# Fourier mixing and an ELU feed-forward on one core: complex product by three real products, units between the halves of the first layer, ELU in halves

## The chip, the cores and the metric

One core of a Trainium2 chip runs one program. The metric is the device time of one execution in microseconds, and the kernel before takes 918.88 us (median of 3 runs, 918.64 to 919.0). The five engines that the text speaks of are PE (TensorE, matmuls, with its weight loads shown as PEld), DVE (VectorE), ACT (ScalarE), POOL (GpSimd) and SP (SyncE, which here only issues transfers).

## The reference

There are 8 batches of 3008 tokens by 256 channels. Each batch goes through a Fourier transform over its tokens, a complex 256x256 matrix product with a bias, soft thresholding, and the inverse transform; then all 24064 tokens go through a two-layer feed-forward with an ELU.

```python
X = rfft(x, axis=1);  Xr, Xi = X.real, X.imag
Yr = Xr @ w_r - Xi @ w_i + b_r
Yi = Xr @ w_i + Xi @ w_r + b_i
Yr = sign(Yr) * max(abs(Yr) - 0.01, 0)      # the same for Yi
y = irfft(Yr + 1j * Yi, n=3008, axis=1)     # (8, 3008, 256)
h = y.reshape(24064, 256) @ w_in            # (24064, 2048)
g = where(h > 0, h, exp(min(h, 0)) - 1)
out = g @ w_out                             # (24064, 256)
```

## The kernel before

**The two parts.** The transform of 3008 = 47 x 64 points is done in stages of matmuls, each followed by a copy out of PSUM. Their pieces are called units. A (`unit_A`, 6 for a batch) is the 47-point stage, written to DRAM (`DA`) and read back as `Z` in another order (`load_Z`). X (`unit_X`, 8) is the 64-point stage, copied to `XT`. M (`unit_M`, 12) is the complex product with the weights. B (`unit_B`, 6) and Y (`unit_Y`, 8) are the inverse stages, with a second trip through DRAM (`DB`, `load_Bs`). Y leaves `yT`, the input of the feed-forward.

**The feed-forward** runs in 376 iterations (47 for a batch). A block is 512 tokens, and 8 iterations go over its 2048 hidden columns, 256 at a time. `front` makes the hidden values of one iteration with 4 matmuls into `hps` (two PSUM banks), ACT takes the exponential into `Et`, DVE or POOL take its minimum, and DVE writes the result to `gT`. Two iterations later (`LAG = 2`) `back` multiplies `gT` by `w_out` with 8 matmuls. `gT` is a ring of three tiles.

**The order of the work** is written out by hand. Batch 0's transform and the tables stand ahead of the loop. Inside it `plan(b)` gives each of the 47 iterations (slots 0 to 46) at most one unit: the late Y of batch b, then X, M and B of batch b+1, A of batch b+2, and the first two Y of batch b+1 (called n). PE runs, for each iteration, the unit (list `f0`), the 4 matmuls of `front`, and the 8 of `back`. A second list, `f1`, holds loads and small steps. In slot 3 of batch 0 it holds `gate`, a POOL copy that waits until `Z` of batch 1 has landed, and the first `load_x` of batch 2 behind it, also issued by POOL.

**Engines of the ELU before.** An iteration without a unit (`free`) has two exponentials of 128x512 on ACT (L735), the minimum in halves on POOL (L763) and two DVE steps (L751). One with a unit other than M has one exponential of 128x1024 (L740), the minimum on DVE (L765) and one DVE step (L753). One with an M has a Relu and an exponential of 128x1024 on ACT (L737, L738) and one DVE step (L751). `psH` holds two tiles of two banks each, and `psF` one of two banks for the units, lent to every third free iteration.

**M before.** For each half of a pair, four matmuls of 512 columns (L193: two for the real part of the input, two for the imaginary, each with [w_r, w_i] or [-w_i, w_r]); DVE adds the bias (L203); POOL clips (L211) and subtracts (L212). Where batches 1 to 7 are meant these are the M inside the loop; batch 0 has its own `first_M`, which the change leaves alone.

**Startup.** `unit_A(1, ...)` runs ahead of the loop and puts two of its three tiles into the slots of the `gT` ring (`shifted`), so that the first writes of `gT` wait until `DA<-A` has been read out.

Of the kernel before, what the change touches and what calls it, by code (L numbers as in the profile page):

```python
# [14 lines left out]

# [8 lines left out]
NJ = 24  # L24
# [5 lines left out]
def kernel(  # L30
# [31 lines left out]
    wcat_s = constp.tile([P, 2, 2 * D], BF16, name="wcat_s")  # L62
    w_in_s = constp.tile([P, 2, DFF], BF16, name="w_in_s")
    w_out_p = constp.tile([P, NFT, E + 16], F32R, name="w_out_r")
    w_out_r = w_out_p[:, :, 0:E]
    bias_bc = constp.tile([P, 2 * D], F32, name="bias_bc")
    bias_p = constp.tile([P, 2 * D], BF16, name="bias_p")
# [11 lines left out]
    zp = ctx.enter_context(tc.tile_pool(name="zp", bufs=1))  # L79
    wk2 = ctx.enter_context(tc.tile_pool(name="wk2", bufs=2))  # L80
# [10 lines left out]
    TB = 512  # L91
# [37 lines left out]

    def unit_A(b, u, alone=False, on_dve=False, ahead=False):  # L130
        ci, uu = u // 2, u % 2
        if uu == 0:
            if ahead and ci > 0:
                A_of[b, ci] = shifted(ci - 1, 8 * D, BF16, "A").rearrange("p (n d) -> p n d", d=D)
# [14 lines left out]
        evac(  # L149
            A[:, 4 * uu : 4 * uu + 4, :].rearrange("p n d -> p (n d)"),  # L150
            ps[:].rearrange("p a b -> p (a b)"), on_dve,
        )
        j0 = 8 * ci
        if alone:
            j0 += 4 * uu
            nc.sync.dma_start(dav[:, j0 : j0 + 4, :], A[:, 4 * uu : 4 * uu + 4, :])
        elif uu == 1:
            nc.sync.dma_start(dav[:, j0 : j0 + 8, :], A[:])
# [8 lines left out]
    def unit_X(b, u, alone=False, on_dve=False):  # L167
# [14 lines left out]
        evac(xv, pv, on_dve)  # L182
# [23 lines left out]

    def unit_M(b, q, i):
        if i == 0:
            mps_of[b, q] = unit_ps("mps", False)
        yb, clip = m_group(b, q, i, mps_of[b, q][:, i, :])  # L210
        nc.gpsimd.tensor_scalar(clip[:], yb, LAM, -LAM, ALU.min, ALU.max)  # L211
        nc.gpsimd.tensor_tensor(Y_of[b, q][:, i, :], yb, clip[:], ALU.subtract)  # L212
# [21 lines left out]
    def unit_B(b, v, alone=False, on_dve=False):  # L234
# [16 lines left out]
        o = 4 * (v % 2)  # L251
        Bv = Bz[:, o : o + 4, :].rearrange("p (q s) d -> p s q d", s=2)
        psv = ps[:].rearrange("p s (q d) -> p s q d", d=D)
        if on_dve:
            nc.scalar.copy(Bv[:, :, 0], psv[:, :, 0])
            nc.vector.tensor_copy(Bv[:, :, 1], psv[:, :, 1])
        else:
            nc.scalar.copy(Bv, psv)  # L258
        if alone:
            k0 = 4 * v  # L260
            nc.sync.dma_start(
                DB_of[b][k0 : k0 + 4].rearrange("k p d -> p k d"), Bz[:, o : o + 4, :]
            )
        elif v % 2:
            k0 = 8 * (v // 2)
            nc.sync.dma_start(DB_of[b][k0 : k0 + 8].rearrange("k p d -> p k d"), Bz[:])
# [8 lines left out]
    def unit_Y(b, u, alone=False, on_dve=False):  # L275
# [11 lines left out]
        evac(  # L287
            yT[:, dt, w * WT : w * WT + WT].rearrange("p (r j) -> p r j", j=8),
            psv[:, :, 0 : 2 * N1].rearrange("p j r -> p r j"), on_dve,
        )  # L290
# [23 lines left out]
    with tc.tile_pool(name="stagep", bufs=1) as stagep:  # L314
# [35 lines left out]
        w_r_f = row("w_r_f", [P, 2, D])  # L350
        w_i_f = row("w_i_f", [P, 2, D])
# [217 lines left out]
    SHIFT = (0, 32, 16)  # L569

    def shifted(k, n_, dt, name):

        k %= 3
        o = SHIFT[k] * n_ // (8 * TB)
        w_ = n_ + 64 * n_ // (8 * TB)
        t = late1.tile([P, w_], dt, name=name, tag=f"gT{k}")
        return t[:, o : o + n_]
# [110 lines left out]
    for u in range(2):  # L688
# [7 lines left out]
        tc.tile_pool(name="psH", bufs=2, space=bass.MemoryType.PSUM, reuse_waits="tile")  # L696
# [19 lines left out]
    def front(i, third, on_act, halves):  # L716
        blk, fp = divmod(i, NPAIR)
        if third:
            hps = psF.tile([P, 2, TB], F32, name="hps", tag="fps")
        else:  # L720
            hps = psH.tile([P, 2, TB], F32, name="hps", tag="hps")
        for s in range(2):
            ft = 2 * fp + s
            for b, t0, c0, c1 in sorted(pieces(blk * TB, TB), key=lambda z: z[3] - z[2]):
                for dt in range(2):
                    nc.tensor.matmul(  # L726
                        hps[:, s, c0:c1], lhsT=w_in_s[:, dt, ft * P : ft * P + P],
                        rhs=yT_of[b][:, dt, t0 : t0 + c1 - c0],
                        start=(dt == 0), stop=(dt == 1),
                    )  # L730
        Et = late3.tile([P, 2, TB], F32, name="Et", tag="Et")
        E_ = Et[:]
        if halves:
            for s in range(2):
                nc.scalar.activation(E_[:, s], hps[:, s], AF.Exp)  # L735
        elif on_act:
            nc.scalar.activation(E_, hps[:], AF.Relu, scale=-1.0)  # L737
            nc.scalar.activation(E_, E_, AF.Exp, scale=-1.0)  # L738
        else:
            nc.scalar.activation(E_, hps[:], AF.Exp)  # L740
        return hps, Et

    late_elu = []

    def finish_elu():
        for i, hps, Et, whole, halves in late_elu:
            gT = shifted(i + 2, 2 * TB, F32R, "gT").rearrange("p (s t) -> p s t", s=2)
            for s in range(2) if halves else (slice(0, 2),):
                o, h, e = gT[:, s], hps[:, s], Et[:, s]
                if whole:  # L750
                    nc.vector.scalar_tensor_tensor(o, e, -1.0, h, ALU.add, ALU.max)  # L751
                else:
                    nc.vector.scalar_tensor_tensor(o, h, 0.0, e, ALU.max, ALU.add)  # L753
            g_of[i] = gT
        late_elu.clear()

    def elu(i, hps, Et, on_pool, on_act):

        E_ = Et[:]
        if on_pool:  # L760
            for s in range(2):
                eng = nc.vector if i == n - 1 and s == 0 else nc.gpsimd
                eng.tensor_scalar(E_[:, s], E_[:, s], 1.0, 0.0, ALU.min, ALU.max)  # L763
        elif not on_act:
            nc.vector.tensor_scalar(E_, E_, 1.0, -1.0, ALU.min, ALU.add)  # L765
        late_elu.append((i, hps, Et, on_pool or on_act, on_pool))

    def back(i, split):
# [24 lines left out]
        for q in range(nq):  # L793
            copy = nc.vector.tensor_copy if (last and q) or (split and q == 0) else nc.scalar.copy
# [16 lines left out]
    def plan(b):  # L811
# [4 lines left out]
        mid = [("X", u) for u in range(8)] + [  # L816
# [4 lines left out]
        ]  # L821
        if n1 < B:
            lead, seq = int(b == 0), [("y", u) for u in range(2, 6)] + mid
            seq.insert(20 if b else 4, ("y", 6))
            seq.insert(24 if b else 5, ("y", 7))
            xs = (3, 8, 13)
            seq += [("A", 5), ("n", 0), ("n", 1)] if b else [("n", 0), ("n", 1), ("A", 5)]
        else:
            lead, seq = 0, [("y", u) for u in range(2, 8)]
        for t, u in enumerate(seq, lead):  # L830
# [7 lines left out]
            else:  # L838
                f0[t].append(put(u[0], n1, *u[1:]))
            if u == ("A", 1):  # L840
                f1[t] += [(load_Bs, (n1, w)) for w in range(4)]
            if u == ("A", 5) and n2 < B:
                f1[t] += [(load_Z, (n2, s0, s1)) for s0, s1 in ((0, 8), (8, NS))]
        if b == 0:
            f1[3].append((scale_w_in, (3, True, 0)))
# [8 lines left out]
    bare = 0  # L854
    for i in range(n + LAG):
        if i < n:
# [4 lines left out]
            free = not used[r]  # L861
            bare = bare + 1 if free else 0
            calm = free and (i >= n - 2 or (r + 2 < PER and not used[r + 1] and not used[r + 2]))
            for f, a in f0[r]:
                f(*a)
            on_act = any(f is unit_M for f, a in f0[r])
            h = front(i, calm and bare % 3 == 1, on_act, free and i > 0)
        finish_elu()
        if i < n:
            for f, a in f1[r]:  # L870
                f(*a)
            split = i > LAG and (i - LAG) % NPAIR == NPAIR - 1
            if split:
                back(i - LAG, True)
            elu(i, *h, free and i > 0, on_act)
        else:
            split = False
        if i >= LAG and not split:
            back(i - LAG, False)
# [30 lines left out]
```

## Time and profile before

| | before |
|---|---|
| median of 3 runs | 918.88 us (918.64 to 919.0) |
| span of the profiled execution | 916.2 us, granted PE clock 0.997 |
| PE busy | 898.2 us (98%) |
| DVE, ACT busy | 718.1 us (78%), 696.8 us (76%) |
| POOL busy | 313.4 us (34%) |
| DMA, mean over the span | 116 GB/s |

The span runs from the first to the last instruction of one profiled execution. No separate time of that execution is listed; the median of the runs is 2.7 us above the span, which is what lies around it. Matmuls are pipelined, so the mean of one (303 ns for L784) is longer than its share of PE; periods between starts of the same kind are the safer reading.

### The profile page before, as it was taken

To read this page: it belongs to the slowest core of one execution; us is meant where nothing else is said; L and a number is where in the kernel's file an instruction comes from. 1 tells how busy PE (TensorE), PEld (TensorE's weight loads), DVE (VectorE), ACT (ScalarE), POOL (GpSimd) and SP (SyncE) were. 2 spreads that over 40 slices of the span, in tenths; PEclk is the share of its full clock that TensorE was granted. 3 is DMA by queue.
4 is the path that set the end of the run, shared out by engine and by line. 5 is a ranking of instruction groups with operands and counts; after the bars stand their busy time and mean duration, and the time that the engine had idled before them with its cause. 6 is when DMAs were issued, how large, how long until landed. Compare 5 with 4: busy or idle time off the path is not lost.

```text
span 916.2 us, 17270 instructions
## 1 busy us (share of the span) xinstructions
PE 898.2 (98%) x6721; PEld 655.8 (72%) x6721; DVE 718.1 (78%) x891; ACT 696.8 (76%) x850; POOL 313.4 (34%) x438
## 2 busy tenths in 40 slices
PE   8889999999999999999999999999999999999997
PEld 3447667876678766886678766787667866777775
DVE  8759778887788777887788877888778877778775
ACT  6658778778778778787787788878877877766664
POOL 6600440323321342405404153033332134343664
PEclk9999999999999999999999999999999999999999
DMA  8997026621284214732266032752228111321011
GB/s 264 310 264 230 24 71 182 210 63 53 70 233 135 71 47 135 191 113 75 65 192 200 24 94 60 218 160 70 70 71 229 30 42 47 87 76 47 26 46 46
DMA packets 90670, 106.24 MB, mean 116 GB/s; under 512 B 5270, under 2 KB 81308, under 8 KB 87228
## 3 DMA queue, kind: packets, MB, share of 16 engines
q1 hardware_dynamic: 84332, 77.62, 30.3%
q0 software_dynamic: 5968, 27.26, 9.0%
q8 instruction: 52, 0.85, 0.4%
q10 hardware_dynamic: 288, 0.26, 0.1%
q14 instruction: 30, 0.25, 0.1%
HBM read 55.32 MB, written 49.81 MB: 115 GB/s over the span
## 4 chain that ended last, share of the span: by engine, by line
PE 88%; DMA 3%; ACT 3%; DVE 3%; issue 1%; SPq 1%; POOL 0%; ACTq 0%; DVEq 0%; POOLq 0%
PE ps_o L784 36%; PE hps L726 34%; PE mps L193 9%; PE xps L176 2%; PE yps L283 2%; PE bps L245 2%; PE aps L145 2%; DMA Bs<-DB 1%; DMA DA<-A 1%; ACT Et L737 1%; ACT Bz L258 1%; SPq L802 0%; DMA xt<-in_x_dram 0%; DVE gT L751 0%; DMA DB<-Bz 0%
## 5 line engine op out<-in xcount | busy, mean ns | idle before, releaser
L784 PE MATMUL ps_o<-w_out_r,gT 128*128 128x256 f32 x3008 | 482.5, 303 | 0.1
L784 PEld LDWEIGHTS ps_o<-w_out_r,gT 128*128 128x128 f32 x3008 | 406.8, 189 | 50.0 <-DVE osb L795 1.0
L726 PE MATMUL hps<-yT,w_in_s 128*128 128x512 bf16 (+4 forms) x1728 | 390.0, 353 | 3.3 <-DVE gT L753 2.5
L751 DVE SCALAR_TENSOR_TENSOR gT<-Et,hps 128x512 fp32r<-128x512 f32 (+1 forms) x272 | 222.8, 848 | 76.3 <-POOL Et L763 39.3
L753 DVE SCALAR_TENSOR_TENSOR gT<-hps,Et 128x1024 fp32r<-128x1024 f32 x198 | 242.1, 1223 | 18.0 <-DMA DA<-A 2.6
L726 PEld LDWEIGHTS <-w_in_s 128*128 128x128 bf16 x1728 | 141.7, 98 | 130.9 <-issue 23.5
L740 ACT ACTIVATE Et<-hps 128x1024 f32<-128x1024 f32 x198 | 203.9, 1030 | 14.3 <-PE hps L726 8.0
L763 POOL TENSOR_SCALAR Et<-Et 128x512 f32<-128x512 f32 x187 | 111.3, 614 | 224.9 <-ACT Et L735 224.9
L765 DVE TENSOR_SCALAR Et<-Et 128x1024 f32<-128x1024 f32 x198 | 137.0, 692 | 49.5 <-ACT Et L740 42.2
L211 POOL TENSOR_SCALAR clip<-yb 128x512 f32<-128x512 f32 x84 | 51.6, 614 | 319.5 <-DVE yb L203 282.1
L735 ACT ACTIVATE Et<-hps 128x512 f32<-128x512 f32 x188 | 102.1, 595 | 65.1 <-PE hps L726 65.1
L737 ACT ACTIVATE Et<-hps 128x1024 f32<-128x1024 f32 x84 | 86.3, 1027 | 72.6 <-PE hps L726 72.1
L212 POOL TENSOR_TENSOR Y<-yb,clip 128x512 bf16<-128x512 f32 x84 | 107.2, 1276 | 7.0
L738 ACT ACTIVATE Et<-Et 128x1024 f32<-128x1024 f32 x84 | 88.8, 1057 | 2.7
L203 DVE TENSOR_TENSOR yb<-mps,bias_bc 128x512 f32<-128x512 f32 x89 | 61.4, 689 | 36.8 <-PE mps L193 29.8
L128 ACT CAST XT<-xps 128x768 bf16<-128x768 f32 x61 | 48.7, 799 | 16.4 <-PE xps L176 16.4
L128 ACT CAST yT<-yps 128x752 bf16<-128x752 f32 x63 | 49.6, 788 | 14.6 <-PE yps L283 14.5
L193 PE MATMUL mps<-wcat_r,XT 128*128 128x512 bf16 x192 | 58.1, 383 | 0.8 <-DVE XT L126 0.4
L128 ACT CAST A<-aps 128x1024 bf16<-128x1024 f32 x45 | 45.5, 1013 | 16.3 <-PE aps L145 14.6
L193 PE MATMUL mps<-wcat_s,XT 128*128 128x512 bf16 x192 | 57.1, 379 | 0.0
L193 PEld LDWEIGHTS <-XT 128*128 128x128 bf16 x384 | 30.8, 98 | 29.9 <-DVE XT L126 0.7
L258 ACT CAST Bz<-bps 128x1024 bf16<-128x1024 f32 x46 | 46.0, 1000 | 2.6 <-PE bps L245 2.6
(110 smaller groups left out, 412.0 us busy)
## 6 DMA issues: line engine op xcount, KB each, us to landing
xt<-in_x_dram POOLq DMA_DIRECT2D x21, 1024.0 KB, 7.1
out_dram<-osb SPq DMA_DIRECT2D x158, 128.0 KB
Bs<-DB SPq DMA_DIRECT2D x32, 384.0 KB
DA<-A SPq DMA_DIRECT2D x21, 512.0 KB
DB<-Bz SPq DMA_DIRECT2D x21, 512.0 KB
Z<-DA SPq DMA_DIRECT2D x7, 1152.0 KB
Z<-DA SPq DMA_DIRECT2D x11, 384.0 KB
xt<-in_x_dram POOLq DMA_DIRECT2D x6, 512.0 KB, 6.2
```

Of the source, the lines that this page charges most:

```text
L128: nc.scalar.copy(dst, src)
L193: nc.tensor.matmul(ps, lhsT=XT[:, dt, c, o : o + P], rhs=wm[:, dt, :], start=(not biased and m == 0 and dt == 0), stop=(m == 1 and dt == 1),)
L212: nc.gpsimd.tensor_tensor(Y_of[b, q][:, i, :], yb, clip[:], ALU.subtract)
L726: nc.tensor.matmul(hps[:, s, c0:c1], lhsT=w_in_s[:, dt, ft * P : ft * P + P], rhs=yT_of[b][:, dt, t0 : t0 + c1 - c0], start=(dt == 0), sto ...
L735: nc.scalar.activation(E_[:, s], hps[:, s], AF.Exp)
L737: nc.scalar.activation(E_, hps[:], AF.Relu, scale=-1.0)
L740: nc.scalar.activation(E_, hps[:], AF.Exp)
L751: nc.vector.scalar_tensor_tensor(o, e, -1.0, h, ALU.add, ALU.max)
L753: nc.vector.scalar_tensor_tensor(o, h, 0.0, e, ALU.max, ALU.add)
L763: eng.tensor_scalar(E_[:, s], E_[:, s], 1.0, 0.0, ALU.min, ALU.max)
L765: nc.vector.tensor_scalar(E_, E_, 1.0, -1.0, ALU.min, ALU.add)
L784: nc.tensor.matmul(po[q][:, i_ % 2, :], lhsT=gT[:, s, i_ * P : i_ * P + P], rhs=w_out_r[:, ft, :], start=(ft == 0 and i_ % 2 == 0), stop=( ...
```

## The change

1. **M by three products.** For batches 1 to 7 the complex product is formed from K = (Xr - Xi) w_i, P = Xr (w_r - w_i) and Q = Xi (w_r + w_i): real part P + K, imaginary part Q + K. That is six matmuls of 256 columns in place of four of 512. The difference Xr - Xi is a new POOL step (`unit_D`, 128x256 in bf16), made two M ahead. DVE adds b_r to K (128x256) and then K to both parts (128x512). POOL adds b_i - b_r to the imaginary part (128x256), then clips and subtracts as before. Three POOL steps in slots 5 to 7 of batch 0 make the sums of the weights and of the bias.
2. **Units between the halves of the first layer.** PE's order in an iteration is now two matmuls of `front`, the unit, two matmuls of `front`, `back`. The unit's copy out of PSUM is issued later (`later`, `flush`): for units other than M between ACT's two exponentials, for M ahead of part of DVE's queue.
3. **ELU in halves.** `psH` holds four tiles of one bank. Each half has its own exponential and its own DVE step. The minimum is on POOL in all iterations without an M, those with X, B, A or Y among them; with an M it is on ACT (two Relu of 128x512, one exponential of 128x1024); in the first 4 iterations it is on DVE. `psF` is for units alone.
4. **Another plan.** X of the next batch begins in slot 5 (batch 0) or 2 in place of 7 or 4; late Y and some A now stand among the M as fill; the slot of n0 goes from 37 to 43 with the batch. Among M0 to M11 stand 4 other slots for batch 1 (worked on in plan 0), 7 for batch 2, 8, 9 and more for later ones. `load_x` moves to slots 1, 4, 7 (batch 0 keeps 3, 8, 13, and `gate` stays in slot 3).
5. **Memory.** `w_out` loses its 16 padding columns and the `gT` ring its shifts; the tiles of `unit_A(1, ...)` move out of the ring. Of each block's two output copies one is always on DVE.

The core of the diff:

```diff
 def unit_M(b, q, i):
+    k = 2 * q + i
+    XT, Xd, o = XT_of[b], Xd_of.pop((b, k)), k * P
+    ps = unit_ps("mps", False)
+    kp = ps[:, 1, 0:D]
+    for lhs, rhs, dst in (
+        (lambda dt: Xd[:, dt], lambda dt: wcat_r[:, dt, D : 2 * D], kp),
+        (lambda dt: XT[:, dt, 0, o : o + P], lambda dt: wsum[:, 0, dt], ps[:, 0, 0:D]),
+        (lambda dt: XT[:, dt, 1, o : o + P], lambda dt: wsum[:, 1, dt], ps[:, 0, D : 2 * D]),
+    ):
+        for dt in range(2):
+            nc.tensor.matmul(dst, lhsT=lhs(dt), rhs=rhs(dt), start=dt == 0, stop=dt == 1)
...
+    def done():
+        nc.vector.tensor_tensor(Kb[:], kp, bias_bc[:, 0:D], ALU.add)
+        nc.vector.tensor_tensor(
+            two(yb[:]), two(ps[:, 0]), Kb[:].unsqueeze(1).to_broadcast([P, 2, D]), ALU.add
+        )
+    def clip_():
+        nc.gpsimd.tensor_tensor(yb[:, D : 2 * D], yb[:, D : 2 * D], bias_d[:], ALU.add)
+        nc.gpsimd.tensor_scalar(clips[0][:], yb[:], LAM, -LAM, ALU.min, ALU.max)
+    def sub_():
+        nc.gpsimd.tensor_tensor(Y_[:, i, :], yb[:], clips[0][:], ALU.subtract)
+    jobs.append((clip_, lambda: unit_D(b, k + 2), sub_))
...
+            h = front_ps()
+            e = Elu(i, h, "dve" if i < 4 else {"M": "act", "F": "pool"}[kind])
+            front_mm(i, h, 0)
             for f, a in f0[r]:
                 f(*a)
+            front_mm(i, h, 1)
+            if was:
+                was.mix(1 if kind == "M" and len(was.todo) == 2 else 0 if kind == "M" else 2)
+            e.exp(0)
+            if kind != "M":
+                flush()
+            e.exp(1)
+            flush()
+            if was:
+                was.mix()
             for f, a in f1[r]:
                 f(*a)
...
+            if kind == "M":
+                for c_, x_, s_ in todo[:-1]:
+                    x_(); s_()
+                todo[-1][0]()
+                jobs.append(todo[-1])
+            else:
+                e.least(0)
+                for c_, x_, s_ in todo: x_()
+                e.least(1)
+                for c_, x_, s_ in todo: s_()
+            e.mix({"MM": 0, "MF": 0, "FM": 1, "FF": 2}[kind + then])
```

Here `x_` is `unit_D` of two M later, `least` the minimum of a half and `mix` the DVE step of a half.

More of the change, by code (lines that the diff above doesn't have):

```diff
@@ L714, in pieces, with front_ps, front_mm @@
         return out_
-    def front(i, third, on_act, halves):
+    def front_ps():
+        return [psH.tile([P, TB], F32, name="hps", tag="hps")[:] for _ in range(2)]
+    def front_mm(i, hps, s):
         blk, fp = divmod(i, NPAIR)
[L718 to L729, printed above, removed]
-                    )
[L731 to L741, printed above, removed]
@@ L757, in elu @@
[L757 to L768, printed above, removed]
+        ft = 2 * fp + s
+        for b, t0, c0, c1 in sorted(pieces(blk * TB, TB), key=lambda z: z[3] - z[2]):
+            for dt in range(2):
+                nc.tensor.matmul(
+                    hps[s][:, c0:c1], lhsT=w_in_s[:, dt, ft * P : ft * P + P],
+                    rhs=yT_of[b][:, dt, t0 : t0 + c1 - c0],
+                    start=(dt == 0), stop=(dt == 1),
+                )
```

254 lines of the change are left out of this document (170 added, 84 removed), and 4 rows, old and new, of the table mid.

## The prediction, made before the changed kernel ran

> **What bounds the kernel now.** I read the page first: busy shares, the chain that ended last, then the groups by form.
>
> ```profile
> PE 898.2 (98%) x6721; PEld 655.8 (72%) x6721; DVE 718.1 (78%) x891; ACT 696.8 (76%) x850; POOL 313.4 (34%) x438
> PE 88%; DMA 3%; ACT 3%; DVE 3%; issue 1%; SPq 1%; POOL 0%; ACTq 0%; DVEq 0%; POOLq 0%
> L212 POOL TENSOR_TENSOR Y<-yb,clip 128x512 bf16<-128x512 f32 x84 | 107.2, 1276 | 7.0
> L211 POOL TENSOR_SCALAR clip<-yb 128x512 f32<-128x512 f32 x84 | 51.6, 614 | 319.5 <-DVE yb L203 282.1 <-PE hps L726 37.4
> L499 POOL TENSOR_TENSOR v<-v,r 128x47 f32<-128x47 f32 x1 | 0.3, 292 | 0.1
> ```
>
> PE sets the time, so PE time that is removed is worth its full length unless a wait takes its place. POOL is idle for two thirds of the span, and its two-input steps are slow (1.28 us for 512 elements).
>
> The timeline gives the period of each sort of iteration, start to start:
>
> ```profile
> 229.10 0.60 PE L193 MATMUL mps<-wcat_r,XT 128*128 128x512 bf16 x2
> 231.79 0.60 PE L193 MATMUL mps<-wcat_r,XT 128*128 128x512 bf16 x2
> ...
> 504.31 1.03 PE L726 MATMUL hps<-yT,w_in_s 128*128 128x512 bf16 x4
> 499.95 1.04 PE L726 MATMUL hps<-yT,w_in_s 128*128 128x256 bf16 x8
> ```
>
> An M iteration takes 231.79 - 229.10 = 2.69 us. By the same reading a free one takes 1.82 (486.05 to 487.87), one with Y or X 2.17, with A 2.29, with B 2.36. The last two lines show that eight matmuls of 256 columns take as long as four of 512: PE pays by the column.
>
> Last the start of the loop, where PE still waits:
>
> ```profile
> 65.32 1.23 DVE L753 SCALAR_TENSOR_TENSOR gT<-hps,Et 128x1024 fp32r<-128x1024 f32 x1 [2.09 <-DMA DA<-A]
> 72.97 0.51 PE L283 MATMUL yps<-M,Bs 96*128 96x94 bf16 x8
> 76.95 0.18 POOL L599 CAST gate<-Z 96x1 f32<-96x1 bf16 x1 [14.88 <-DMA Z<-DA]
> 77.44 1.83 POOL L117 DMA_DIRECT2D xt<-in_x_dram  x3 [0.32 <-issue]
> 58.00:60.00 2.00, 2.00 (x12) 1.07 (x11) 0.00 (x0) 0.65 (x1) 0.00 (x0) 0.50 1.06 298
> ```
>
> POOL sits in `gate` until 76.95, and nobody minds, since nothing of POOL's is needed so early. The last line is a stretch of 2 us with the granted clock in its third column from the end: half.
>
> **1. M by three products, on PE.** M costs 2.69 - 1.82 = 0.87 us; six times 256 columns are three quarters of four times 512, so 0.22 is saved, 84 times: **-18.3**.
>
> **2. The start: POOL's gate now stands ahead of the ELU.** Iteration 4 is the first whose minimum is on POOL, and POOL reaches it only after slot 3, that is after `gate` and one `load_x`. What `gate` waits for does not move: the same transfers in the same SP order stand ahead of `Z`. So: gate 76.95, issue from 77.44 for 1.83 / 3 = 0.61 to 78.05, first half of the minimum 0.61 to 78.66, DVE's half 0.69 (a row of L751) with a hand-over of 0.03 to 79.38. Only then is the bank free that iteration 6 writes first, and PE, DVE and SP stand behind it. Before, PE stood at that same point (units y2 to y5 and one more done, iteration 6 next) at 72.97: 6.4 lost. The gain that the moved tiles of A would bring (DVE's 2.09 us in the first line) comes before that stall and is swallowed by it, and so is any wait of X0 in slot 5 for the first part of `Z`. Behind the gate the two weight sums (two-input, 512 elements, 1.28 each) delay the minima of iterations 5 and 6: iteration 7 can start at 79.25 + 1.28 + 0.61 + 0.72 = 81.86, against 79.38 + 2.17, iteration 8 likewise: 0.6 in all. After 6 us without work PE's clock should be half for a time, as in the line at 58 to 60 (with its neighbours about 3.4 us at half, at most 1.7 us of work lost); POOL holds PE back there anyway, so I take 0.5 between 0 and 1.7. Sum **+7.5**.
> The Trainium skill, "TensorE: Matmul & The Clock Gate", Part 1, says that an idle window of about 3.4 us halves the clock until a window of work has passed. The trace agrees (0.50 at 58 to 60); by that rule alone this item would be 1.2 more.
>
> **3. POOL among the M of batch 1.** Two-input POOL rows: 292 ns at 47 elements, 1276 at 512, so 2.12 ns an element and 0.73 us at 256. Each M then asks POOL for the difference 0.73, the bias 0.73, the clip 0.61, the subtraction 1.28, and 0.08 between dependent steps (7.0 / 84 in L212): 3.43, where PE needs 2.69 - 0.22 = 2.47. Twelve M put POOL 12 x 0.96 = 11.5 us behind. An iteration without M asks POOL for 1.20 (two halves, back to back) and gives back 1.16 (B) or 0.97 (Y). For batch 1 only four B stand among the M: -4.6. The first two differences are made earlier (-1.5), M11's subtraction delays nothing among them (-1.3), and a difference may be 0.9 late: after an M's matmuls DVE needs 1.11, POOL 1.42 and 0.73, together 3.3, and the M after next wants it 4.3 later. Left: **+3.2**. For batch 2 four B and three Y give back 7.5, and 11.5 - 7.5 - 3.7 = **+0.3**. Later batches have more fill: 0.
> The difference is bf16 in and out, which no two-input row shows. Half the fp32 rate per byte gives 0.45, the price of 512 elements 1.28; the row of L212 already writes bf16 at the fp32 slope, so I take 0.73 and keep both for the range.
>
> **4. Units between the halves.** One more change of kind on PE for each of some 270 units. A costs 2.29 - 1.82 = 0.47 against 0.43 for two matmuls of 512: at most 0.02 for a change, 0 to 5.5; **+1.5**, since X and Y show almost none. ACT runs exponential, unit copy, exponential: 1.19 + 1.01 = 2.20 in the worst case (A), below 2.29, and 2.25 (two Relu of 0.595, L738's 1.06) in an M iteration, below 2.47: hidden; where ACT has an output copy of 0.58 as well, it runs late for an iteration and eats slack. The bank pairs come free within about 2.8 us of a half's matmuls (0.60 + 0.61 + 0.69 and a unit's copy of at most 1.01), and PE returns to them after 3.6 or more: hidden. DVE falls to two halves of 0.69 for most iterations (1.38 of 1.82 or more), with 0.42 + 0.69 for an M: hidden, and `psF` is free 1.1 us after an M's matmuls, 0.7 before the next unit.
>
> **5. The rest.** `load_Bs` of batch 1 is issued two slots earlier against its use, which takes away PE's wait of 0.7 at 151 (a Y for `Bs<-DB`): **-0.7**. Padding and ring shifts: no row shows `back` without them; between rows of one tile place and another `back`'s pace differs by about 1 ns in 118, so 0 +- 3. The last iteration's minimum is no longer split with DVE, hidden by DVE's own half: 0.
>
> Sum on the span: 916.2 - 18.3 + 7.5 + 3.2 + 0.3 + 1.5 - 0.7 = 909.7. With the 2.7 us around it (918.88 - 916.2): **912.4**.
>
> **Rivals.**
> *POOL is dearer, and it is slower.* Place: the M stretches; price: each 0.1 us more on POOL per M costs about 1.2 in batch 1 and 2 each, and less in later ones as fill absorbs it. At 0.2 more (3.63 in all) it is 2.4 + 2.4 + 1.7 + 0.6 = 7, and the gain is gone: this is the point that decides. At 0.3 more it is near 13, so about **924**. For it: the sum stands 5% below the turning point, and two steps of four have no row of their own. Against: rows at 1, 47 and 512 elements lie on a line. Chance 0.2.
> *POOL is cheaper or the start is mild.* The difference at 0.45 takes away item 3 (-3.4): 909; if also PE lost only half of item 2, **905**. For it: bf16 has half the bytes. Against: `gate`'s place in POOL's order is plain. Chance 0.15.
> *ACT becomes the bound.* Halves cost 2 x 0.595 against 1.03 (L735, L740), 0.16 more. In A and B iterations ACT would have 2.2 of 2.3 us; with 0.1 more for each hand-over in 78 of them it is 8 us: **920**. Against: in the trace two halves back to back take 1.08, not 1.19. Chance 0.08.
> The Trainium skill, "Advanced Engine Details and Errata", The Read-Write Bubble, advises instructions of 512 or 1024 elements, because latency is exposed between instructions; it speaks against the halves, and this rival is what it would do here.
> *The saving is not made*, because six weight loads in place of four set PE's pace: PEld's 98 ns for one (L726, bf16) lies under the 0.87 / 8 = 109 ns of 256 columns, so hardly; it would give 912 + 18 = 930, chance 0.02.
>
> **How the numbers follow.** Forecast 0.55, the cases above 0.45. 0.2% (1.8 us) is about what a measurement can tell from no change. Faster by more: 0.51 of the forecast's 0.55 (its spread, from items 2 to 5, is some 906 to 919) and the cheap case's 0.15, 0.66. The same: the forecast's other 0.04, 0.04 of the POOL case and 0.03 of ACT's, 0.11. Slower: the other 0.16 and 0.05 of these two, and 0.02 of the last, 0.23. The range runs from the cheap case to the dear one: 904 to 923.
>
> **What would show it.** PE's M iteration at 2.47 us; POOL at 600 us or more, with rows near 0.73 for the difference and the bias; PE idle for some 6 us before iteration 6's first matmul at about 79.4, released by DVE behind POOL's `gate`; waits of M on the difference in batch 1 (100 to 135 us), few in batch 3 and later. It is wrong if the difference's row is above 0.9, if the stall at 73 to 79 is absent, or if PE waits for ACT throughout.

## The result, and the profile after

The changed kernel takes 906.06 us (median of 4 runs, 905.47 to 907.28); the kernel before, on the same chip, 918.82. The ratio is 0.9864, with a 95% interval of 0.985 to 0.9878. The forecast was 912.4, with a range of 904 to 923. The profiled execution has a span of 904.2 us and took 905.97. For the kernel before no time of the profiled execution is on record; in its later runs, which have both, the time is 1.7 to 1.9 us above the span, so its 916.2 belong to a run of some 918.0. The 2.7 us taken as lying around the span were about 0.9 too many.

The page of the changed kernel, busy shares and the chain that ended last:

```profile
PE 873.7 (97%) x6778; PEld 668.6 (74%) x6889; DVE 654.7 (72%) x1066; ACT 709.6 (78%) x1132; POOL 664.8 (74%) x998
PE 84%; POOL 6%; issue 4%; DVE 3%; DMA 2%; ACT 1%; SPq 0%; ACTq 0%; DVEq 0%; POOLq 0%
```

PE still carries the chain, but POOL, at 0% of it before, now has 6%. POOL's busy time went from 313 to 665 us. Where it went, by the groups of the changed kernel (busy time and mean ns of one behind the bar, then the idle time ahead of them):

```profile
L813 POOL TENSOR_SCALAR Et<-Et 128x512 f32<-128x512 f32 x576 | 351.1, 617 | 166.7 <-ACT Et L808 165.7
L278 POOL TENSOR_TENSOR Y<-yb,clip 128x512 bf16<-128x512 f32 x84 | 108.4, 1290 | 0.3
L274 POOL TENSOR_TENSOR yb<-yb,bias_d 128x256 f32<-128x256 f32 x84 | 61.6, 734 | 13.3 <-DVE yb L266 12.4
L240 POOL TENSOR_TENSOR Xd<-XT 128x256 bf16<-128x256 bf16 x84 | 56.3, 673 | 0.0
L275 POOL TENSOR_SCALAR clip<-yb 128x512 f32<-128x512 f32 x84 | 51.7, 615 | 7.4
```

An M costs POOL 0.673 + 0.734 + 0.615 + 1.290 + 0.09 (7.4 / 84, the gap ahead of the clip) = 3.40 us; the prediction had 3.43. The two rows that it had to draw from a line, 0.73 each, came out at 0.734 in fp32 and 0.673 in bf16.

PE's timeline after, an iteration with M and then, after the dots, one without a unit:

```profile
215.84 0.39 PE L790 MATMUL hps<-yT,w_in_s 128*128 128x512 bf16 x1
216.29 0.38 PE L256 MATMUL mps<-wcat_r,Xd 128*128 128x256 bf16 x2
216.50 0.60 PE L256 MATMUL mps<-wsum,XT 128*128 128x256 bf16 x4
218.31 0.60 PE L790 MATMUL hps<-yT,w_in_s 128*128 128x512 bf16 x2
...
477.81 1.04 PE L790 MATMUL hps<-yT,w_in_s 128*128 128x512 bf16 x3
479.61 1.04 PE L790 MATMUL hps<-yT,w_in_s 128*128 128x512 bf16 x4
```

From first half to first half the M iteration takes 218.31 - 215.84 = 2.47 us, as forecast. The free one takes 1.80; before it was 1.82, and nothing in the sum of the prediction stood for that.

The start of the loop in the timeline after, first PE (in brackets the idle time ahead and what ended it):

```profile
73.03 0.82 PE L192 MATMUL xps<-M,Z 96*128 96x96 bf16 x8 [5.91 <-DMA Z<-DA]
80.29 1.01 PE L790 MATMUL hps<-yT,w_in_s 128*128 128x512 bf16 x2 [3.88 <-DVE gT L825]
```

The same stretch of the timeline, POOL:

```profile
77.79 0.18 POOL L665 CAST gate<-Z 96x1 f32<-96x1 bf16 x1 [16.74 <-DMA Z<-DA]
78.29 0.56 POOL L115 DMA_DIRECT2D xt<-in_x_dram  x1 [0.32 <-issue]
78.88 1.21 POOL L813 TENSOR_SCALAR Et<-Et 128x512 f32<-128x512 f32 x2
```

And two stretches of 2 us from the view by windows (busy time of PE, PEld, DVE, ACT and POOL, then the granted clock, the DMA share and GB/s):

```profile
72.00:74.00 2.00, 0.97 (x9) 0.77 (x10) 0.00 (x0) 0.11 (x1) 0.00 (x0) 0.50 0.99 227
82.00:84.00 2.00, 2.00 (x9) 1.75 (x8) 1.10 (x2) 1.38 (x2) 2.00 (x3) 0.50 0.32 123
```

PE stands twice: 5.91 us for the first part of `Z`, which X0 in slot 5 needs, and then 3.88 us for DVE's half of iteration 4, whose minimum waits on POOL behind `gate` until 78.88. Iteration 6 starts at 80.29 (forecast 79.4). The granted clock, third from the end, is at half in both stretches. By the records it is so from 71.1 to 84.8.

**Where the time went.** A period is the time from the last matmul of one `back` to that of the next. A batch here is the 47 iterations of one plan, so batch 0's M are those that the prediction calls M of batch 1. For each kind of iteration I take the median over batches 1 to 7, before and after:

| kind (number of such iterations) | before | after |
|---|---|---|
| M (84) | 2.687 | 2.467 |
| B (42) | 2.458 | 2.479 |
| A (36) | 2.290 | 2.294 |
| X (56), Y (60) | 2.170, 2.166 | 2.147, 2.140 |
| without a unit (95) | 1.823 | 1.800 |

Medians times numbers change by -22.5 us. What the periods take beyond their medians, PE's waits mostly, goes from 7.9 to 21.1: in batch 0 from 3.2 to 16.5 (13.7 of it in the iterations of X0 to X2), in batches 1 to 7 from 4.8 to 4.6. The first `back` ends 2.1 earlier (a figure of one execution: in the ten variants of the changed kernel below it ends between 62.2 and 64.2, here at 62.3), and -0.3 is left for the tail. The sum is -11.8, and the spans differ by 12.0.

### The profile page after: what moved, and what is told of

It is laid out like the page before. It is cut to its first block, busy times and chain, and to the rows that moved or that the text cites. A ratio compares the mean times of both kernels' runs of the same rounds, so it can differ in the third digit from the quotient of the medians.

```text
span 904.2 us, 18246 instructions
## 1 busy us (share of the span) xinstructions
PE 873.7 (97%) x6778; PEld 668.6 (74%) x6889; DVE 654.7 (72%) x1066; ACT 709.6 (78%) x1132; POOL 664.8 (74%) x998
## 4 chain that ended last, share of the span: by engine, by line
PE 84%; POOL 6%; issue 4%; DVE 3%; DMA 2%; ACT 1%; SPq 0%; ACTq 0%; DVEq 0%; POOLq 0%
PE ps_o L845 36%; PE hps L790 32%; PE mps L256 5%; PE bps L314 3%; PE xps L192 2%; PE aps L158 2%; PE yps L355 2%; POOL Y L278 1%; PE mps L209 1%; POOL yb L274 1%; POOL Et L813 1%; POOL Xd L240 1%; POOL clip L275 1%; DMA Bs<-DB 1%; DMA xt<-in_x_dram 1%
## 5 line engine op out<-in xcount | busy, mean ns | idle before, releaser
L825 DVE SCALAR_TENSOR_TENSOR gT<-Et,hps 128x512 fp32r<-128x512 f32 x752 | 496.9, 684 | 193.6 <-POOL Et L813 168.7
L813 POOL TENSOR_SCALAR Et<-Et 128x512 f32<-128x512 f32 x576 | 351.1, 617 | 166.7 <-ACT Et L808 165.7
L790 PE MATMUL hps<-yT,w_in_s 128*128 128x512 bf16 (+7 forms) x1622 | 418.6, 354 | 6.2 <-DVE gT L825 4.7
L808 ACT ACTIVATE Et<-hps 128x512 f32<-128x512 f32 x584 | 341.7, 603 | 103.3 <-PE hps L790 98.9
L804 ACT ACTIVATE Et<-hps 128x512 f32<-128x512 f32 x168 | 100.6, 599 | 51.9 <-PE hps L790 46.8
L274 POOL TENSOR_TENSOR yb<-yb,bias_d 128x256 f32<-128x256 f32 x84 | 61.6, 734 | 13.3 <-DVE yb L266 12.4
L266 DVE TENSOR_TENSOR yb<-mps,Kb 128x512 f32<-128x512 f32 x84 | 58.1, 692 | 3.0
L240 POOL TENSOR_TENSOR Xd<-XT 128x256 bf16<-128x256 bf16 x84 | 56.3, 673 | 0.0
L265 DVE TENSOR_TENSOR Kb<-mps,bias_bc 128x256 f32<-128x256 f32 x84 | 35.5, 423 | 27.9 <-PE mps L256 27.7
L256 PE MATMUL mps<-wsum,XT 128*128 128x256 bf16 x336 | 50.4, 273 | 0.0
L192 PEld LDWEIGHTS <-Z 96*128 96x128 bf16 x512 | 29.2, 99 | 22.5 <-DMA Z<-DA 7.4
L192 PE MATMUL xps<-M,Z 96*128 96x96 bf16 x512 | 33.0, 208 | 9.0 <-DMA Z<-DA 6.2
```

The lines of the kernel that those rows point to most:

```text
L192: nc.tensor.matmul(psv[:, kk, 0 : 4 * K1], lhsT=Z[:, k, dt * P : dt * P + P], rhs=M2[:, k].rearrange("p c m -> p (c m)"), start=True, stop ...
L256: nc.tensor.matmul(dst, lhsT=lhs(dt), rhs=rhs(dt), start=dt == 0, stop=dt == 1)
L274: nc.gpsimd.tensor_tensor(yb[:, D : 2 * D], yb[:, D : 2 * D], bias_d[:], ALU.add)
L790: nc.tensor.matmul(hps[s][:, c0:c1], lhsT=w_in_s[:, dt, ft * P : ft * P + P], rhs=yT_of[b][:, dt, t0 : t0 + c1 - c0], start=(dt == 0), sto ...
L804: nc.scalar.activation(e, h, AF.Relu, scale=-1.0)
L808: nc.scalar.activation(e, h, AF.Exp)
```

## The experiments

My theory: the products by three are worth 0.22 us an M on PE, the start gives some 9 us back, POOL's lag some 2 to 3 us in batch 0's M, and the padding and shifts that were taken away make `back` faster. Rivals: `back` is faster for another reason; POOL's lag costs more than is seen; the order of units, not the products, made the gain. The ELU in halves and the plan behind its start were not undone by themselves, so what they are worth alone is not shown.

**The kernel before without padding and shifts.**

```diff
-    w_out_p = constp.tile([P, NFT, E + 16], F32R, name="w_out_r")
-    w_out_r = w_out_p[:, :, 0:E]
+    w_out_r = constp.tile([P, NFT, E], F32R, name="w_out_r")
...
-    SHIFT = (0, 32, 16)
+    SHIFT = (0, 0, 0)
...
-        w_ = n_ + 64 * n_ // (8 * TB)
+        w_ = n_
```

> The kernel before, with w_out in rows of 256 columns (no 16 of padding) and all three gT slots at offset 0. Theory: the pace of back comes from where its two operands lie in SBUF, so back's period in a free iteration falls from 1.823 us towards the 1.800 of the changed kernel, 376 times 0.023, about 8 us: 910 to 911. Rival: the pace comes from what DVE, ACT and POOL do beside it (the halves of the ELU), so nothing moves: 918 to 919.5.

914.78 us, ratio 0.9945 (0.9926 to 0.9964). Its timeline, two free iterations:

```profile
483.81 1.04 PE L725 MATMUL hps<-yT,w_in_s 128*128 128x512 bf16 x4
485.61 1.04 PE L725 MATMUL hps<-yT,w_in_s 128*128 128x512 bf16 x4
```

1.80 instead of 1.82: the place of these tiles moves `back`'s pace, in a kernel that has nothing else of the change. By medians and numbers the place is worth 6.2 us. The time moved by 4 to 5, and the span of the profiled execution by 3.2: what its periods take beyond their medians grew by 4, 2.6 of it in batch 0, mostly in the late Y.

**The changed kernel with padding and shifts, and with the padding alone.**

```diff
+    w_out_p = constp.tile([P, NFT, E + 16], F32R, name="w_out_r")
+    w_out_r = w_out_p[:, :, 0:E]
-    w_out_r = constp.tile([P, NFT, E], F32R, name="w_out_r")
```

and, in the first of the two only, the shifts of the `gT` ring.

> The changed kernel, with the 16 padding columns of w_out and the shifts of the gT ring put back. Theory (place in SBUF sets the pace of back): the free period goes back from 1.800 to about 1.823, and the time from 906 to about 914. Rival (the halves of the ELU set it): no change, 905.5 to 907.

> The changed kernel with the padding of w_out's rows put back (1088 bytes from row to row in place of 1024), the three slots of gT without their shifts as in the change. It parts the two halves of the place effect (padding and shifts together moved a free iteration from 1.800 to 1.829 us and the time by some 4 us). If the rows of w_out set it: a free iteration at 1.82 to 1.83, 909.5 to 911 us. If the shifts of gT set it: 1.800, 905.5 to 907 us. Both equally likely to me.

Both: 910.69 us, ratio 0.9908 (0.9886 to 0.993). Padding alone: 910.21 us, ratio 0.99 (0.9882 to 0.9918). Against the 0.9864 of the changed kernel that is 4.0 and 3.3 us. Free iterations in the timeline with both:

```profile
479.38 1.04 PE L795 MATMUL hps<-yT,w_in_s 128*128 128x512 bf16 x4
481.20 1.04 PE L795 MATMUL hps<-yT,w_in_s 128*128 128x512 bf16 x4
```

And in the timeline with the padding alone:

```profile
478.64 1.04 PE L791 MATMUL hps<-yT,w_in_s 128*128 128x512 bf16 x4
480.46 1.04 PE L791 MATMUL hps<-yT,w_in_s 128*128 128x512 bf16 x4
```

1.82 each time. So the padding, with rows of `w_out` 1088 bytes apart in place of 1024, slows `back`, and the shifts beside it do nothing that shows; the shifts without the padding were not run. The padding also makes the tile larger, which may move the tiles behind it, so that the distance of the rows is what counts is argued, not shown. Between matmuls of `back` the mean step is 116.4 ns without the padding, 118.3 with it and 118.7 with both. Medians times numbers give 7.1 us for padding and shifts. The times give less, because the waits beyond the medians fall by 2.7 when PE is slower.

**The start moved.**

```diff
-        early = 6 if b == 0 else 4
+        early = 7 if b == 0 else 4
...
-        xs = (3, 8, 13) if b == 0 else (1, 4, 7)
+        xs = (9, 11, 13) if b == 0 else (1, 4, 7)
```

X0 goes to slot 6, `gate` and the first `load_x` to slot 9.

> The changed kernel; in batch 0 the X of the next batch begin in slot 6 in place of 5, and POOL's gate and the first load_x stand in slot 9 in place of 3, the second load_x in 11. Theory: the stall at 67 to 85 us (9.1 us against the kernel before, after back(4)) is POOL's gate ahead of the minimum of iteration 4, and Z landing at 73 for X0; without the gate in its place PE still waits for Z, but loses only about 0.5 against the kernel before: 906 - 8.6 = about 897.5, and no granted clock of 0.5 after 72 us for more than one stretch. Rival: Z alone sets the start, since X0 and X2 need it whatever POOL does: at most 2 us better, 904 to 906.

898.03 us (896.68 to 899.71), ratio 0.9768 (0.9745 to 0.9791): faster than both kernels, 8 us below the changed one. PE in its timeline:

```profile
72.44 0.52 PE L192 MATMUL xps<-M,Z 96*128 96x96 bf16 x8 [2.34 <-DMA Z<-DA]
75.31 1.08 PE L790 MATMUL hps<-yT,w_in_s 128*128 128x512 bf16 x2
```

POOL in the same timeline:

```profile
81.02 0.18 POOL L665 CAST gate<-Z 96x1 f32<-96x1 bf16 x1
```

And two stretches of 1 us from its view by windows, columns as above:

```profile
73.00:74.00 1.00, 1.00 (x4) 0.73 (x3) 0.04 (x1) 0.96 (x2) 0.00 (x0) 0.50 0.88 221
77.00:78.00 1.00, 1.00 (x10) 0.95 (x9) 0.24 (x1) 1.00 (x3) 0.62 (x1) 1.00 0.00 0
```

One stand of 2.34 us is left in place of 5.91 and 3.88, `gate` finds its data at once, and iteration 7 begins at 75.31, before iteration 6 did in the changed kernel. The lead is 8.7 us behind iteration 7 and some 9 until the last B of the batch, which in this plan stands for POOL's last subtraction:

```profile
139.56 0.39 PE L314 MATMUL bps<-Y,M 64*128 64x256 bf16 x4 [1.69 <-POOL Y L278]
```

From there 7.4 us stay to the end. The start term of the prediction is real and can be had back by two numbers of the plan. They were moved together, so what X0's slot and `gate`'s slot are worth one by one is not shown.

**Four products again.** The changed kernel with the four matmuls of 512 columns, without POOL's difference and bias step, with one DVE addition.

```diff
-        for lhs, rhs, dst in (
-            (lambda dt: Xd[:, dt], lambda dt: wcat_r[:, dt, D : 2 * D], kp),
...
+        for m, (c, wm) in enumerate(((0, wcat_r), (1, wcat_s))):
+            for dt in range(2):
+                nc.tensor.matmul(
+                    ps[:, 0, :], lhsT=XT[:, dt, c, o : o + P], rhs=wm[:, dt, :],
```

> The changed kernel with M of batches 1 to 7 by the four products of 512 columns again: the difference Xr - Xi, the bias step on POOL and DVE's 128x256 step are left out, clip and subtraction stay on POOL, all else as changed. Theory: PE pays 0.22 us more for each of 84 M (18.3), and the 2 to 3 us that batch 1's M wait for POOL go away: 906 + 16 = about 922, with an M iteration of 2.69 us. Rival (the gain of the change lies in the interleaving and the halves, and the three products only move work to POOL): less than 5 us of difference, 906 to 911.

917.9 us, ratio 0.9988 (0.9976 to 1.0). An M iteration in its timeline:

```profile
217.75 0.61 PE L782 MATMUL hps<-yT,w_in_s 128*128 128x512 bf16 x2
220.43 0.61 PE L782 MATMUL hps<-yT,w_in_s 128*128 128x512 bf16 x2
```

2.68 us, so three products are worth 2.682 - 2.467 = 0.215 by the medians, 84 times 18.1. The time moves by 11.4 only (0.9988 - 0.9864, times 918.8): with four products nothing waits in batch 0's M, and the waits of batches 1 to 6 are 0.9 us where the changed kernel has 4.4. About a third of what PE saves on M is spent waiting around M. Without the three products the change would have been worth nothing that can be told from no change: what the place of the tiles gives is about what the start takes.

**POOL with more work on M, and with less.**

```diff
+            nc.gpsimd.tensor_tensor(spare[:], bias_bc[:, 0:64], bias_bc[:, 64:128], ALU.add)
```

> The changed kernel with one more two-input instruction of 64 columns on POOL in each M of batches 1 to 7 (into a tile that nobody reads), by the rows of this trace some 0.32 us: POOL's work for an M goes from 3.40 to 3.72 us, where PE takes 2.47. Theory (the prediction's sum of POOL's lag in the M stretches, with a turning point at 3.63): about 4 us more in batch 1, 4 in batch 2 and 4 in the others, 918 us (913 to 922). Rival (POOL's lag is taken up by the fills between the M and by the two differences made ahead, so the M stretches are bound by PE): 906 to 908 us, the same as the changed kernel.

```diff
-            nc.gpsimd.tensor_tensor(yb[:, D : 2 * D], yb[:, D : 2 * D], bias_d[:], ALU.add)
```

> The changed kernel without POOL's addition of the bias difference to the second half of M of batches 1 to 7 (that addition is left out of the computation): POOL's work for an M falls from 3.40 to 2.67 us, 0.2 above PE's 2.467. It asks how much of the changed kernel's time is still owed to POOL's work on M. Theory (the waits of batch 0's M, 2.3 us over their median, and B's 0.3 after them are POOL's; those of later batches, 4.6 in all, hardly: 0.32 us more on POOL moved only batches 0 to 2): 3 us less, 903 us (902 to 904.5). Rival (nearly all waits after the start are POOL's, as the kernel with four products lost them all): 899 to 901 us.

More: 910.04 us, ratio 0.99 (0.9886 to 0.9915). Less: 903.01 us, ratio 0.9819 (0.9802 to 0.9836). The group that was added, in the first:

```profile
L275 POOL TENSOR_TENSOR spare<-bias_bc 128x64 f32<-128x64 f32 x84 | 27.0, 321 | 0.0
```

The clip's group in the second, with its idle time at the end:

```profile
L274 POOL TENSOR_SCALAR clip<-yb 128x512 f32<-128x512 f32 x84 | 51.5, 613 | 21.9 <-DVE yb L266 20.3
```

0.32 us more on POOL for each M costs 3 to 4 us, not the 12 that the prediction's sum gave, and no turn is seen at 3.63. Batch 0's M go from 2.66 to 2.86 on average, and two Y in batch 1 and an A in batch 2 wait some 0.7 more each; batches 3 to 7 don't move. With 0.73 less, POOL's wait for DVE's sums grows (20.3 us in the last line, against 12.4 ahead of L274 in the changed kernel), and the time falls by 3 us by the medians and 4 by the ratios; the profiled execution shows 1.8 of it in batch 0 and 0.4 in batch 1. So POOL's lag is real, but some 2 to 4 us in all. Theory held for the smaller load, and missed the larger by two thirds.

The waits of batches 2 to 6 stay as they were, so they aren't POOL's. The trace names another engine for half of the 4.4 us of batches 1 to 6. 2.2 lie in four iterations that each follow a block's output copies (the first is in batch 2, the others in batch 6), and in all four `back` begins 0.05 us after ACT's copy ends. That copy stands behind the exponential of an M. ACT in the timeline of the changed kernel:

```profile
760.05 1.06 ACT L806 ACTIVATE Et<-Et 128x1024 f32<-128x1024 f32 x1
761.01 0.57 ACT L856 COPY osb<-ps_o 128x512 f32<-128x512 f32 x1
```

PE in the same timeline:

```profile
761.63 1.21 PE L845 MATMUL ps_o<-w_out_r,gT 128*128 128x256 f32 x8 [0.26 <-ACT osb L856]
```

With four products, where an M lasts 0.21 us longer, 0.5 of the 2.2 is left. Of the rest 0.4 went with POOL's bias step, and the cause of some 1.8, in pieces of 0.2 and less, stays open.

What the lag looks like in the chain of waits of the changed kernel, in batch 0's M (pieces in order of time, some between them left out):

```profile
119.06 1.24 POOL Y L278
120.30 0.70 POOL yb L274
121.08 0.61 POOL clip L275
122.28 0.64 POOL Xd L240
123.50 1.25 POOL Y L278
```

From 117.8 to 130 POOL follows POOL without a gap, and two M in a row start 2.77 apart (121.43 and 124.20) instead of 2.47.

**Units ahead of both halves.**

```diff
-            front_mm(i, h, 0)
             for f, a in f0[r]:
                 f(*a)
+            front_mm(i, h, 0)
             front_mm(i, h, 1)
```

> The changed kernel with one thing put back: a unit's matmuls stand ahead of both halves of the first layer, not between them. Theory (the order of the units on PE is worth little; a change of kind costs PE some 0.03 us where the unit's matmuls use part of the rows): B iterations 2.479 to about 2.44, A 2.294 to about 2.27, Y, X and M as they are, and no new waits, since the banks of both halves come free well before the next iteration's use: some 3 us less, 903 us (900 to 906.5). Rival (the place between the halves is needed to spread the bank pairs, so that PE would wait for DVE's half before each iteration with a unit): 0.05 us or more in each of some 270 iterations, 915 to 925 us, seen as PE's waits on the mix ahead of the first half.

952.35 us, ratio 1.0362 (1.0347 to 1.0378): neither theory nor rival had this. ACT in its timeline:

```profile
537.82 0.60 ACT L808 ACTIVATE Et<-hps 128x512 f32<-128x512 f32 x1
538.31 0.79 ACT L126 CAST XT<-xps 128x768 bf16<-128x768 f32 x1
```

PE in the same timeline:

```profile
539.16 0.33 PE L192 MATMUL xps<-M,Z 96*128 96x96 bf16 x4
```

The unit's matmuls are over before ACT can start the exponential of the first half, but its copy stands behind that exponential in ACT's queue. It ends at 538.31 + 0.79 = 539.10, and the next unit, which has only this one PSUM tile, starts at 539.16. X goes from 2.147 to 2.313, A from 2.294 to 2.763, M from 2.467 to 2.818. I had undone half of a pair: the unit's place on PE and its copy's place on ACT belong together.

**Units first, and their copies first.** `flush()` moved up behind the units, ahead of both halves and exponentials.

> The changed kernel with a unit's matmuls ahead of both halves of the first layer, and this time the unit's copies ahead of the exponentials as well (both in the order that the kernel before had; the minimum in halves and M by three products as changed). It is to tell what of the 46 us that units first cost with the copies left behind the exponential came from the copies. Theory (the one bank of the units has to be copied out before the next unit, so the copy must not stand behind an exponential that waits for a half issued after the unit): the waits are gone, A, B and M iterations lose one change of kind, 0.015 us each in the steps between matmuls (hps after ps_o 231 ns against 216 after hps), 162 x 0.015 = 2.4: about 904 us (902 to 907), X and Y at 2.14. Rival (the halves themselves have to stand apart): 912 us or more, with waits of the first half on DVE's mix or of the back on gT.

912.31 us, ratio 0.9924 (0.9909 to 0.994): 40 of the 46 us came from the copy, and the rest is 5.5 us by the ratios. A and B do gain what a change of kind costs (2.260 against 2.294, 2.456 against 2.479), but PE's waits for M's sums are more: ahead of M by the two lines below, and ahead of B and Y 2.1 us against 0.4. From its view of waits (us in total, times, longest):

```profile
PE mps L256 <- DVE yb L266: 3.6, 9, 0.7
```

The same line in the view of waits of the changed kernel:

```profile
PE mps L256 <- DVE yb L266: 0.9, 2, 0.6
```

What the periods of batches 1 to 6 take beyond their medians goes from 4.4 to 9.9 us, as much as the 5.5. Free iterations are at 1.820 here, as in the kernel with the units alone first, 0.02 slower (1.9 us in all) though neither edit moves a tile, which I can't explain; it offsets what A and B gain. So the rival had the size, though PE waits for the sums of M and not for the mix: units between the halves are worth some 5 us.

**The minimum on DVE**, in all iterations without M, and in those between a batch's first and last M alone (this with the moved start).

```diff
-            e = Elu(i, h, "dve" if i < 4 else {"M": "act", "F": "pool"}[kind])
+            e = Elu(i, h, "dve" if i < 4 else {"M": "act", "F": "dve"}[kind])
```

```diff
+            among = "M" in kinds[:r] and "M" in kinds[r:]
+            e = Elu(i, h, "dve" if i < 4 else "act" if kind == "M" else "dve" if among else "pool")
```

> The changed kernel with the minimum of every iteration without M on DVE in place of POOL (0.425 us for a half in the rows of iterations 0 to 3). Theory (POOL carries the minimum because DVE can't): DVE then has 2 x (0.683 + 0.425) = 2.22 us in an iteration, PE 1.80 where there is no unit and 2.14 with Y or X; some 95 free iterations lose 0.42 and some 110 with Y or X lose 0.08, +49 us in all, less some 10 us that POOL's gate at the start and its waits in the M stretches no longer cost: about 945 us (930 to 955), and a start without the 6 us stall. Rival (DVE evens out over neighbouring iterations, as three tiles of E and three of gT allow; its sum of 655 + 245 = 900 us stays below PE's): 895 to 910 us.

> The kernel with the moved start (first part of X of batch 1 in slot 6, gate and load_x from slot 9) and, beside it, the minimum of the iterations without M that stand between the first and the last M of a batch on DVE in place of POOL. Theory (what is left of PE's waits at those iterations, about 4 us over batches 0 to 6, and some 2 us in batch 0's M, comes from POOL, which falls behind by 0.93 us in each M and wins back only 0.97 to 1.25 in an iteration whose minimum it makes): without the minimum it wins back 2.1 to 2.5, and the time goes from 898.0 to about 893 us (891 to 896). Rival (the waits there are the mix's place in DVE's order, not POOL's lag): 898 us as without it, or up to 901 where DVE's 2.2 us in such an iteration delays the sums of an M.

966.71 us, ratio 1.0535 (1.0508 to 1.0563), and 935.68 us, ratio 1.0187 (1.017 to 1.0204). Both far worse than expected; the second gave up 38 us of the moved start's 898. The group of the minimum among the M, in the second:

```profile
L815 DVE TENSOR_SCALAR Et<-Et 128x512 f32<-128x512 f32 x128 | 114.1, 923 | 2.3 <-ACT Et L808 2.3
```

0.923 us, where the expectation had the 0.425 of iterations 0 to 3 (8 of these 128 are those). DVE in the timeline of the first kernel shows why:

```profile
559.81 0.45 DVE L815 TENSOR_SCALAR Et<-Et 128x512 f32<-128x512 f32 x1
560.49 1.17 DVE L815 TENSOR_SCALAR Et<-Et 128x512 f32<-128x512 f32 x1 [0.24 <-ACT Et L808]
```

POOL in the same timeline:

```profile
559.93 1.45 POOL L278 TENSOR_TENSOR Y<-yb,clip 128x512 bf16<-128x512 f32 x1
```

DVE's first half is under way when POOL's subtraction begins, and that takes 1.45 in place of 1.28: it runs to 561.38. DVE's second half begins at 560.49 and ends at 561.66, 0.28 after POOL. So the later one stands for most of the other's time. Of the 585 minima of that kernel the 457 beside no POOL instruction take 0.42 us on average, and the 53 beside a subtraction alone 1.37. The Trainium skill, "SBUF — State Buffer", the section "SBUF: two separate sides", says that DVE in its faster modes and POOL take a common pair of SBUF ports in turn, each holding it for a whole instruction; these lines agree. DVE's sums and halves of M read PSUM and show no such stretch (L266 0.692 in both kernels). And DVE had no room anyhow: an M costs it 0.42 + 0.69 + 2 x 0.68 = 2.48 of PE's 2.467. PE's waits then move to the B above all, which go from 2.479 to 2.94 and 2.95.

## Why the prediction came out as it did

The direction and the range held, and the mechanism was as told but for one term; the forecast was 6.3 us too high, 5.5 on the span and 0.8 in what was taken to lie around it. The medians of the changed kernel with padding and shifts (M 2.481, B 2.475, A 2.309, free 1.829) part the order of the work from the place of the tiles. Step by step, on the span:

| item | forecast | measured | from |
|---|---|---|---|
| 1, M by three products | -18.3 | -17.3 | (2.687 - 2.481) x 84; 18.1 by the kernel with four products |
| 2, start | +7.5 | +8.7 | batch 0's waits +13.4, less 2.6 of its M and B, less 2.1 for the earlier first `back` |
| 3, POOL among the M | +3.5 | +2.4 | batch 0's M and B +2.6; later batches -0.2 against before |
| 4, change of kind | +1.5 | +2.0 | (2.475 - 2.458) x 42, 0.019 x 36, 0.006 x 95 |
| 5, wait for `Bs` | -0.7 | in items 2 and 3 | PE's waits for `Bs` fell from 2.7 to 0.6 in all |
| 5, padding and shifts | 0 ± 3 | -7.1 | medians of the two changed kernels times numbers |

The measured column sums to -11.3; the span lost 12.0, and 0.5 of the 0.7 left lies behind the last period that was counted.

- **The mis-sized term is item 5**, the padding and shifts. The prediction saw that `back`'s pace differs by about 1 ns in 118 between places, and left the sign open. It is about 2 ns in 118, on the side of the change in all three kernels that part it, for eight matmuls in each of 376 iterations. The times of those kernels put it at 3 to 5 us, the medians at 6 to 7, beyond the prediction's own 3; either way it is half of the 6.3 or more.
- **Item 1** was right as it stood: PE pays by the column, and six weight loads in place of four don't hold it.
- **Item 2** had the right place, cause and nearly the right size. Two parts were low: `gate` came 0.84 later than before (77.79 against 76.95), and the clock cost more than the 0.5 taken: at half from 71.1 to 84.8, of which PE works some 4.5 us after 80.29 and so loses about 2.2. With these two the sum would have been 10, against 8.7: the sums of the weights, taken at 0.6, lie in the slow stretch and cost nothing beside it, and batch 0's wait for `Bs`, 0.7, is gone in this row. The Trainium skill, "TensorE: Matmul & The Clock Gate", Part 1, gives an idle window of about 3.4 us as what halves the clock. The stands of 5.91 and 3.88 agree. With the moved start 2.34 us without work was enough (0.50 from 73), less than that page says, and the half clock at 58 to 60, in which the prediction saw agreement, follows stands of 1.08 and 0.54 us only. The last section has what the traces show in its place.
- **Item 3** had POOL's price for an M right (3.40 against 3.43) and its bill a little high. It took 2.36 us for an iteration with B, which is the step from a B's start to the next unit's; its period is 2.458, so four B give back 0.4 more. But the turning point at 3.63, on which the rival of a dear POOL rested, does not exist as priced: 3.72 costs 3 to 4 us, not 12. The sum let every M's lag reach PE. In fact it reaches PE while POOL follows POOL without a gap, which is batch 0's stretch; in later batches the fills take it up, as the prediction said for batch 3 on.
- **Item 4** was right in the change of kind and blind to its other side: with the units between the halves the M's sums come in time, which is worth some 5 us against units first. It also let ACT's output copies eat slack only; behind an M they cost the 2.2 us above.
- **What would show it** came out on each point: M at 2.47, POOL at 665, rows near 0.73, a stall before iteration 6, waits in batch 0's M. Only the stall came as two.
- ACT as the bound throughout is not seen: PE's waits on it are below 1 us in any group, and the 2.2 us above are all that the periods show of it. The page that this rival named, the Trainium skill's "Advanced Engine Details and Errata", The Read-Write Bubble, advises 512 or 1024 elements, so it doesn't speak against halves of 512.

## What to carry to other kernels

Before a step is moved to an idle engine, list what else stands in that engine's queue there: `gate`, harmless before, and an X that now comes too early for its data cost 8 us together once POOL had work that PE waits for, and two numbers in the plan took them back. A saving on the bound engine is worth its full length only while the others keep up: 18 us on PE became 11, because an M costs POOL 3.40 and DVE 2.48 of PE's 2.47, and ACT's output copies behind an M come late. POOL's minimum could not be moved to DVE, which has no room and stands while POOL subtracts. When an order is undone in an experiment, undo its partner as well, here the copy on ACT that belongs to the unit on PE.

## What the runs showed of the hardware

- With rows of `w_out` 1088 bytes apart, in place of 1024, fp32r matmuls of 256 columns step by about 118 ns in place of 116.4, though each instruction reads a contiguous row. Shifts of the other operand by 16 and 32 bytes beside that do nothing that shows. That the padding counts is shown; why it does is not, and free iterations at 1.820 without any padding (units first, with and without their copies) say that place is not the whole of it.
- DVE's fp32 minimum of 512 elements within SBUF takes 0.42 us alone and 1.37 on average beside POOL's two-input subtraction, which takes 1.39 where a minimum overlaps it and 1.28 where none does (the kernel with the minimum on DVE throughout).
- POOL's two-input price is by the element, hardly by the byte: 256 elements take 0.734 in fp32 and 0.673 in bf16.
- The granted clock changes only at steps of 3.41 us. In the 13 traces of this case there are some 3440 such steps; PE's busy share of each is reckoned from its matmul rows. From full the clock went to half after every step with a share of 0.45 or less, after some with 0.47 to 0.55 and after none with more. From half it came back after a step with 0.84 or more, and stayed after one with 0.83 or less. Two examples: with the moved start the step from 69.43 to 72.84 has 0.31, and the clock is half until 76.26; in the kernel before the step from 54.27 to 57.68 has 0.52, and the clock is half until 61.09, though the longest stand in it is this one:

```profile
56.01 0.84 PE L283 MATMUL yps<-M,Bs 96*128 96x94 bf16 x16 [1.08 <-DMA Bs<-DB]
```
